# Three real products for a complex one, and an inverse transform in 64-row products over two row groups

## The chip, the cores and the metric

The kernel runs on one core of one Trainium2 chip. The metric is the time of one execution on the device, in microseconds: the median of several runs. TensorE (PE) multiplies matrices out of SBUF into PSUM, VectorE (DVE), ScalarE (ACT) and GpSimd (POOL) do elementwise work, and SyncE (SP) issues most DMAs.

## The reference

```python
def _attn_ref(x, w_r, w_i, b_r, b_i):            # x: 8 x 2496 x 256
    X = np.fft.rfft(x, axis=1)
    Yr = Xr @ w_r - Xi @ w_i + b_r               # w_r, w_i: 256 x 256
    Yi = Xr @ w_i + Xi @ w_r + b_i
    Yr = np.sign(Yr) * np.maximum(np.abs(Yr) - lam, 0.0)      # lam = 0.01, Yi alike
    y = np.fft.irfft(Y, n=x.shape[1], axis=1)
```

The result, 19968 rows of 256, goes through a mixture of 8 experts: logits `y @ w_gate`, a greedy assignment by falling logit with 2496 places for each expert, and for each expert `relu(h @ w1) @ w2` (256 to 1024 to 256).

## The kernel before, in words

The transform of 2496 = 39 x 64 points is done as matrix products, batch by batch (8 batches), in `phase_a`:

- **Stage 1** (L1063, in the last batch L1067): the 39-point transform, 11 units `u` a batch, each three products of 512 columns into a bank `p15`; ScalarE copies it out (L1083) and a DMA stores it in DRAM (`T1`).
- **Stage 2** (L1107): the 64-point transform. A step `p` (10 a batch, 80 in all) takes two frequencies k1 = 2p, 2p+1; for each, two products put the spectrum, transposed, into `ps2`: 256 channels in two halves of 128 partitions, with 64 columns of real parts and 64 of imaginary parts. The table `Ft` is the moving operand.
- Each fp32 value is then split into a high and a low fp32r part, `th` and `tl` (tiles `xTh`, `xTl`): ScalarE writes `th` (L1116), VectorE the rest `tl` (L1117). The negated imaginary part is put ahead of the real one (L1118 on ScalarE, L1119 on VectorE), so that a window of 128 columns reads (Xr, Xi) or (-Xi, Xr).
- **Stage 3** (L1126) is the complex product. For each of the two frequencies 12 products of 256 columns sum into one half of `ps3`: for w_r and w_i, for two channel halves, the three terms high-high, high-low, low-high. The 128 output partitions are 64 real and 64 imaginary rows of one frequency.
- VectorE adds the bias in place (L1132), ScalarE and VectorE apply the threshold (L1133, L1134), and the result is split again into `zh` (ScalarE, L939) and `zl` (GpSimd, L942).
- **Stage 4** (L1142): the inverse 64-point transform. For each frequency three products of 128 rows and 256 columns (table halves `Gt` high and low, data `zh` and `zl`) sum into a half of `ps4`; one ScalarE copy (L1144) and a DMA to `T2` in DRAM.
- **Stage 5** (L1173, from batch 5 on L1177): the inverse 39-point transform of the batch before, 11 units a batch, again in `p15`, copied by ScalarE (L1178), stored as rows of y. Four transposes (L1196) and small gate products (L1214, 32 columns of the array each) give the logits.

A planner (`Plan`) sets the order on every engine. Each task has an engine, a cost, a due place `pos` (10 per batch), the buffers that it reads and writes; a simulation of its own takes the task that can start first, and the instructions are emitted in that order. Rings of buffers (`RINGS`) say how many tiles a kind has: `p15=2, ps2=2, ps3=2, ps4=1`. So the work of several batches and stages is interleaved on each engine, and every engine takes its instructions strictly in the order emitted. An early part of the routing for the first half of the rows (`R.early`, L423 and L727 to L790) is planned between the places 52.5 and 78, on VectorE mostly. After the last batch the experts follow (L624 transposes, L639 first layer, L656 second layer), with the rest of the routing on VectorE beside them.

At the start, 32 products of 64 rows (L1079) run on a tile of zeros; they keep TensorE busy until data arrives and compute nothing:

```python
for i in range(2 * WARM):
    for r in range(2): T.matmul(psw[r].t, lhsT=zr.t[64 * r:64 * r + 64, 0:128], rhs=zr.t[64 * r:64 * r + 64], ...)
```

## Time and profile before

| | |
|---|---|
| runs of the kernel | 1554.78, 1556.19, 1557.17 us; median 1556.19 |
| the profiled execution | 1560.31 us, of which its span 1558.5 |
| granted TensorE clock, mean | 0.995 |
| busy | PE 1524.0, DVE 1063.4, ACT 854.4, POOL 670.0 us |
| stage 3 products | 1920, between 31.0 and 564.6 us |
| stage 4 products | 480, between 40.2 and 572.1 us |

The span runs from the first to the last instruction of the profiled execution; the rest of its time lies around it. Busy time is the union of the records of an engine. A record of PE has a modelled end, and records overlap, so the pace of products is read from one start to the next. The transform takes the first 620 us or so, and the experts the rest.

### The profile page before, as it was taken

What the parts mean: (1) busy time and instruction counts of PE and PEld (TensorE: products, weight loads), DVE (VectorE), ACT (ScalarE), POOL (GpSimd) and SP (SyncE); (2) the same over time, 40 slices, a digit from 0 to 9 for tenths busy, and PEclk for the clock granted to TensorE, in tenths of its full rate; (3) what the DMA queues carried; (4) which work ended last, traced back from release to release, by engine and by line L of the source; (5) the groups of instructions that cost most, each with busy time, mean ns of one, the idle gap of its engine ahead of it and who ended that gap; (6) DMA issues with size and microseconds to landing.
All of it is one profiled execution on the core that took longest, in us unless ns stands there. A gap on an engine that the chain in (4) does not pass through costs nothing.

```text
span 1558.5 us, 31615 instructions
## 1 busy us (share of the span) xinstructions
PE 1524.0 (98%) x10991; PEld 1363.4 (87%) x10991; DVE 1063.4 (68%) x3452; ACT 854.4 (55%) x1870; POOL 670.0 (43%) x891
## 2 busy tenths in 40 slices
PE   7999999999899999999999999999999999999998
PEld 5999999998878877888788998988988889989997
DVE  3676667676975574889989888897777765552321
ACT  2778888787678776444536234344353443552332
POOL 2246556564536444343334434334324343353332
PEclk9999999999999999999999999999999999999999
DMA  9678777877758566434213122121211212311110
GB/s 272 193 243 257 221 248 219 254 240 225 228 172 269 168 205 191 150 114 131 91 43 101 45 69 72 47 89 53 89 44 54 88 57 71 117 51 47 41 47 29
DMA packets 144201, 208.25 MB, mean 134 GB/s; under 512 B 28751, under 2 KB 108575, under 8 KB 144030
## 3 DMA queue, kind: packets, MB, share of 16 engines
q1 hardware_dynamic: 127244, 162.30, 33.9%
q0 software_dynamic: 16656, 43.77, 9.0%
q8 instruction: 89, 1.46, 0.4%
q14 instruction: 82, 0.67, 0.1%
q10 hardware_dynamic: 130, 0.06, 0.0%
HBM read 121.31 MB, written 84.75 MB: 132 GB/s over the span
## 4 chain that ended last, share of the span: by engine, by line
PE 79%; DVE 7%; issue 5%; DMA 4%; ACT 3%; POOL 2%; SPq 0%; POOLq 0%; DVEq 0%; ACTq 0%
PE ps L656 25%; PE ps L639 18%; PE ps L1126 10%; PE p L639 6%; PE ps L1107 4%; PE ps L1142 3%; PE p L1063 2%; PE p L1173 2%; PE ps L624 2%; PE both L1196 2%; PE p L1177 1%; DVE junk L423 1%; POOL out_dram L664 1%; PE ps L1214 1%; DMA sh<-in_x_dram 1%
## 5 line engine op out<-in xcount | busy, mean ns | idle before, releaser
L1126 PE MATMUL ps<-wt,xTh 128*128 128x256 f32 x1280 | 243.6, 288 | 2.2 <-DVE y L1134 1.1
L1126 PEld LDWEIGHTS ps<-wt,xTh 128*128 128x128 f32 x1280 | 198.8, 189 | 10.5 <-issue 5.9
L1126 PE MATMUL ps<-wt,xTl 128*128 128x256 f32 x640 | 178.9, 280 | 0.3 <-DVE xTl L1119 0.3
L664 POOL DMA_INDIRECT out_dram<-xTh,li x64 | 66.0, 1031 | 254.1 <-ACT xTh L660 218.9
L423 DVE SCALAR_TENSOR_TENSOR junk<-h_m,st,h_AG 128x156 bf16<-128x156 f32 (+1 forms) x472 | 160.8, 385 | 2.7
L942 POOL TENSOR_TENSOR zl<-y,zh 128x512 fp32r<-128x512 f32 x80 | 106.4, 1330 | 119.2 <-ACT zh L939 106.1
L1203 POOL TENSOR_TENSOR yTl<-yr,yTh 128x468 bf16<-128x468 f32 (+1 forms) x88 | 96.9, 1103 | 117.7 <-ACT yTh L1202 113.6
L1126 PEld LDWEIGHTS ps<-wt,xTl 128*128 128x128 f32 x640 | 120.5, 188 | 0.5 <-DVE xTl L1119 0.5
L656 PE MATMUL ps<-FG,yTh 128*128 128x256 f32 (+1 forms) x472 | 107.4, 282 | 0.0
L664 POOL DMA_INDIRECT out_dram<-xTl,li x64 | 65.3, 1020 | 91.9 <-ACT xTl L660 75.9
L1107 PE MATMUL ps<-FG,sh 128*128 128x128 f32 x640 | 98.0, 281 | 4.8 <-DMA sh<-T 4.3
L1107 PEld LDWEIGHTS ps<-FG,sh 128*128 128x128 f32 x640 | 87.3, 194 | 13.4 <-DMA sh<-T 4.8
L660 ACT COPY xTl<-ps 128x256 f32<-128x256 f32 x80 | 29.8, 372 | 126.0 <-PE ps L656 96.5
L660 ACT COPY xTh<-ps 128x256 f32<-128x256 f32 x80 | 29.9, 374 | 123.0 <-PE ps L656 95.6
L942 POOL TENSOR_TENSOR s2l<-s2c,s2h 120x512 fp32r<-120x512 f32 (+2 forms) x60 | 77.1, 1288 | 42.6 <-DVE s2h L939 31.1
L656 PE MATMUL ps<-FG,y 128*128 128x256 f32 x408 | 84.7, 282 | 0.0
L942 DVE TENSOR_TENSOR xl<-xt,xh 117x512 fp32r<-117x512 f32 (+1 forms) x66 | 65.4, 992 | 24.9 <-ACT xh L939 22.9
L1117 DVE TENSOR_TENSOR xTl<-ps,xTh 128x512 fp32r<-128x512 f32 x80 | 54.8, 685 | 40.0 <-ACT xTh L1116 39.3
L656 PEld LDWEIGHTS ps<-FG,yTh 128*128 128x128 f32 (+1 forms) x472 | 77.8, 186 | 1.1
L656 PE MATMUL ps<-FG,s1st 128*128 128x256 f32 (+1 forms) x356 | 74.2, 284 | 0.0
L656 PE MATMUL ps<-FG,yst 128*128 128x256 f32 x328 | 72.6, 282 | 0.0
L1201 DVE TENSOR_TENSOR yr<-both,yTh 128x468 f32<-128x468 f32 (+1 forms) x77 | 48.1, 625 | 35.9 <-ACT yTh L1200 33.0
(699 smaller groups left out, 5054.7 us busy)
## 6 DMA issues: line engine op xcount, KB each, us to landing
xt<-in_moe_w_dram SPq DMA_DIRECT2D x64, 512.0 KB
T<-s4st SPq DMA_DIRECT2D x80, 256.0 KB
sh<-T SPq DMA_DIRECT2D x39, 512.0 KB
s2c<-T SPq DMA_DIRECT2D x80, 240.0 KB
YD<-yst SPq DMA_DIRECT2D x80, 234.0 KB
T<-s1st SPq DMA_DIRECT2D x73, 240.0 KB
xt<-in_x_dram SPq DMA_DIRECT2D x105, 156.0 KB
sh<-in_x_dram SPq DMA_DIRECT2D x14, 156.0 KB
```

Source lines behind the costliest of these rows:

```text
L423: v(cols + 59 + 1400 * K.extra, p, lambda k=k: V.scalar_tensor_tensor(junk[k % 2].t[:, 0:cols], H.m[:, 0:cols], c.t[:, k // ng:k // ng + 1 ...
L639: T.matmul(ps.t[:, 0:w], lhsT=W1.t[:, a, m, 128 * ft:128 * ft + 128], rhs=x_.t[:, 0:w], start=q + m == 0, stop=q + m == 3)
L656: T.matmul(ps.t[0:M], lhsT=a.t[:, 128 * q:128 * q + M], rhs=W2.t[:, w_, ft], start=k == 0, stop=k == 23)
L660: plan.add('A', .27, pos + 1, lambda: A.copy(o.t[0:M], ps.t[0:M]), [ps], [o])
L664: ins = P.indirect_dma_start(out=self.out, out_offset=bass.IndirectOffsetOnAxis(ap=oi.t[0:M, oo + t:oo + t + 1], axis=0), in_=o.t[0:M], in ...
L942: lambda: eng.tensor_tensor(lb[1](), src(), hb[1](), op=OP.subtract), [srcb, hb[0]], [lb[0]])
L1107: T.matmul(ps.t[:, i, 128 * dt:128 * dt + 128], lhsT=sh.t[:, k, 128 * dt:128 * dt + 128], rhs=Ft.t[:, k], start=True, stop=True)
L1117: plan.add('V', dve(512), pos, lambda th=th, tl=tl, src=src, apart=apart: apart(V.tensor_tensor(cols(tl, 64, 192), src(), cols(th, 64, 192 ...
L1126: T.matmul(ps3.t[:, i], lhsT=a.t[:, i, dt, o:o + 128], rhs=wt[c].t[:, w, dt], start=n == 0, stop=n == 11)
L1142: T.matmul(ps4.t[:, i], lhsT=Gt[p // 8].t[:, g, (2 * p + i) % 16], rhs=v.t[:, i], start=n == 0, stop=n == 2)
L1201: plan.add('V', dve(2 * W), pos + 0.376, lambda yh=yh, yr=yr, psT=psT, W=W: V.tensor_tensor(yr.t[:, :, 0:W], psT.t[:, :, 0:W], yh.t[:, 0, ...
L1203: yq.append(plan.add('P', pool(2 * W), pos + 0.376, lambda yh=yh, yl=yl, yr=yr, W=W: P.tensor_tensor(yl.t[:, :, 0:W], yr.t[:, :, 0:W], yh. ...
```

## The change

Stage 3 computes with three real products in place of four. With S = Xr + Xi it forms Xr (w_i - w_r), S w_r and -Xi (w_r + w_i); then Yr is the second plus the third, Yi the second plus the first. Each is a group of 6 products of 256 columns (two channel halves, three terms) for both frequencies of the step at once: the 128 stationary columns are now 64 of one frequency and 64 of the other. The groups go into the two halves of `ps3`: the first into half 1; the second into half 0; VectorE reads half 0 out into `sk`, with b_i added (L1150), and only then the third group sums onto half 0. Two adds of VectorE finish: b_r to half 0 (L1157), `sk` to half 1 (L1158). S itself is formed from the two split parts: an add on VectorE (L1135), a second one of two SBUF operands (L1137, on GpSimd for even steps and on VectorE for odd ones; batch 0 all on VectorE), then split by ScalarE (L1138) and GpSimd (L1139). The negated part and its split go away. The weight sums are formed once at the start, with one more split (tile kinds `w3h`, `w3l`).

So real and imaginary parts of both frequencies now lie in the two halves of one tile, and stage 4 takes 64 rows at a time: 12 products a step in place of 6, alternating between the rows 0 to 63 (first frequency, one bank) and 64 to 127 (second frequency, another bank); two copies of 256 columns in place of one of 512. The table `Gt` is arranged to suit, through the stationary columns of `Ft`, which stage 2 now reads as two pieces of 64 columns.

To hold this, `ps4` has two banks and `p15` one (with `ps4` in its place for every second unit of the last batch), some buffers are laid out anew, and `R.early` is planned from place 52.5 to 98.

The core of the diff:

```diff
-            th, tl = sb("xTh", [128, 2, 2, 192], F32R), sb("xTl", [128, 2, 2, 192], F32R)
+            th, tl = sb("xTh", [128, 3, 4, 64], F32R), sb("xTl", [128, 3, 4, 64], F32R)
...
-                        T.matmul(ps.t[:, i, 128 * dt:128 * dt + 128], lhsT=sh.t[:, k, 128 * dt:128 * dt + 128], rhs=Ft.t[:, k], start=True, stop=True)
+                        T.matmul(ps.t[:, 2 * dt + i], lhsT=sh.t[:, k, 128 * dt:128 * dt + 128], rhs=Ft.t[:, k // 2 * 2:k // 2 * 2 + 2, 64 * (k % 2):64 * (k % 2) + 64], start=True, stop=True)
...
-            plan.add('A', act(256, False), pos + .01, lambda th=th, apart=apart: apart(A.mul(cols(th, 0, 64), cols(th, 128, 192), -1.0)), [th_], [th])
-            plan.add('V', dve(256), pos + .01, lambda th=th, tl=tl, src=src: V.tensor_tensor(cols(tl, 0, 64), cols(th, 128, 192), src(64), op=OP.subtract), [ps, th_], [tl])
+            plan.add('V', dve(256), pos + .01, lambda th=th, sq=sq, src=src: V.tensor_tensor(sq(), src()[:, 0], th.t[:, 1].bitcast(F32), op=OP.add), [ps, th_] + ([Bsk] if b + p else []), [Bk] + ([] if b + p else [Bsk]))
+            s1_, s2_ = vb(), vb()
+            plan.add(*(('V', dve(256)) if p % 2 or not b else ('P', pool(256))), pos + .01, lambda tl=tl, sq=sq, e=(P, V)[p % 2 or not b]: e.tensor_tensor(sq(), sq(), tl.t[:, 1].bitcast(F32), op=OP.add), [Bk, tl_], [s1_], uses=[Bsk, Bk])
+            plan.add('A', act(256, False), pos + .02, lambda th=th, sq=sq: A.copy(th.t[:, 2], sq()), [s1_], [th, s2_], uses=[Bsk, Bk])
+            plan.add(*(('P', pool(256)) if b else ('V', dve(256))), pos + .02, lambda th=th, tl=tl, sq=sq, e=P if b else V: e.tensor_tensor(tl.t[:, 2], sq(), th.t[:, 2].bitcast(F32), op=OP.subtract), [s1_, s2_], [tl, sl_], uses=[Bsk, Bk])
...
-                                T.matmul(ps3.t[:, i], lhsT=a.t[:, i, dt, o:o + 128], rhs=wt[c].t[:, w, dt], start=n == 0, stop=n == 11)
+                            T.matmul(ps3.t[:, o], lhsT=a.t[:, x_, 2 * dt:2 * dt + 2].rearrange("p q k -> p (q k)"), rhs=w_at[w_](w)[:, dt], start=n == 0 and k < 2, stop=n == 5, skip_group_check=k == 2)
...
+                if k == 2:
+                    Bk2 = vb()
+                    plan.add('V', dve(256), pos + .8, lambda ps3=ps3, sk=sk: V.tensor_tensor(sk(), ps3.t[:, 0], Bbt.t[:, 1], op=OP.add), [b0, Bbt], [Bk, Bk2], uses=[ps3, Bsk])
+                    need = [Bk2]
+                plan.add('T', .71, pos + .7 + .15 * k, mm3, need + w_of[w_], [ps3, got], uses=[th, tl])
...
-            plan.add('V', dve(512), pos + 1.282, lambda ps3=ps3: V.tensor_tensor(ps3.t, ps3.t, bt[:, None, :].to_broadcast([128, 2, 256]), op=OP.add), [ps3, Bbt], [yb], uses=[ps3])
+            plan.add('V', dve(256), pos + 1.282, lambda ps3=ps3: V.tensor_tensor(ps3.t[:, 0], ps3.t[:, 0], Bbt.t[:, 0], op=OP.add), [ps3, Bbt], [yb], uses=[ps3])
+            plan.add('V', dve(256), pos + 1.282, lambda ps3=ps3, sk=sk: V.tensor_tensor(ps3.t[:, 1], ps3.t[:, 1], sk(), op=OP.add), [ps3, Bk2], [yb], uses=[ps3, Bsk, Bk])
...
-                for i in range(2):
-                    for n, (g, v) in enumerate(((0, zh), (0, zl), (1, zh))):
-                        T.matmul(ps4.t[:, i], lhsT=Gt[p // 8].t[:, g, (2 * p + i) % 16], rhs=v.t[:, i], start=n == 0, stop=n == 2)
+                for n in range(6):
+                    c, (g, v) = n % 2, ((0, zh), (1, zh), (0, zl))[n // 2]
+                    for i in range(2):
+                        T.matmul(ps4[i].t, lhsT=Gt[p // 8].t[64 * i:64 * i + 64, g, (2 * p + c) % 16], rhs=v.t[64 * i:64 * i + 64, c], start=n == 0, stop=n == 5)
...
-                 FG=2, fg=1, wt=2, eq=1, T1=2, T2=2, p15=2, ps2=2, ps3=2, ps4=1, pt=1, pc=1, lo=1, hs=6, ho=1,
+                 FG=2, fg=1, wt=2, eq=1, T1=2, T2=2, p15=1, ps2=2, ps3=2, ps4=2, pt=1, pc=1, lo=1, hs=6, ho=1,
...
-                R.early(Pos(52.5, 78, 128), Ft)
+                R.early(Pos(52.5, 98, 128), Ft)
```

What this makes of the order on PE. Before, a stretch of the first batch: stage 2 (L1107), a whole stage 4 (L1142), then the two weights of one frequency in stage 3 (`wt_367` is w_r, `wt_372` is w_i), one right behind the other.

```order
L1107 MATMUL ps_1374<-FG_238,sh_1050 128x128 x2
L1142 MATMUL ps_1377<-zh_1338,FG_359 128x256
L1142 MATMUL ps_1377<-zl_1356,FG_359 128x256
L1142 MATMUL ps_1377<-zh_1338,FG_359 128x256 x2
...
L1126 MATMUL ps_1388<-wt_367,xTh_1314 128x256 x2
L1126 MATMUL ps_1388<-wt_367,xTl_1334 128x256
...
L1126 MATMUL ps_1388<-wt_372,xTh_1314 128x256 x2
L1126 MATMUL ps_1388<-wt_372,xTl_1334 128x256
```

Now, in a steady batch, the second group (`wt_367`, w_r) and the third (`wt_379`, the weight sum) of one step, into the same `ps_2271`:

```order
L1146 MATMUL ps_2271<-wt_367,xTh_2246 128x256 x2
L1146 MATMUL ps_2271<-wt_367,xTl_2256 128x256
...
L1126 MATMUL ps_2319<-FG_237,sh_2119 128x128 x2
L1082 MATMUL p_2365<-xh_2287,d_94 120x512
L1082 MATMUL p_2365<-xl_2315,d_94 120x512
...
L1146 MATMUL ps_2271<-wt_379,xTh_2246 128x256 x2
L1146 MATMUL ps_2271<-wt_379,xTl_2256 128x256
```

Between the two groups the planner has put half a stage 2 (L1126 in the new numbering) and a unit of stage 1 (L1082), the time in which VectorE reads the bank out.

Stage 4 in the new order on PE, between a unit of stage 5 (L1200) and stage 2: `ps_2297` and `ps_2298` are the banks of the two frequencies.

```order
L1200 MATMUL p_2283<-s2h_2159,d_95 39x256
L1169 MATMUL ps_2297<-zh_2254,fg_563 128x256
L1169 MATMUL ps_2298<-zh_2254,fg_563 128x256
...
L1169 MATMUL ps_2297<-zl_2266,fg_563 128x256
L1169 MATMUL ps_2298<-zl_2266,fg_563 128x256
...
L1126 MATMUL ps_2319<-FG_237,sh_2119 128x128 x2
```

The 12 products of a step stand together, the two row groups in turn, with products of the whole array ahead of them and behind.

VectorE around the same step, in the new order. L1150 is the read-out of `ps_2271`, L1137 an add of two SBUF operands, L953 the low part of a stage-1 input (also two SBUF operands):

```order
L1133 TENSOR_TENSOR xTl_2295<-ps_2258,xTh_2279 128x512
L1135 TENSOR_TENSOR sk_411<-ps_2258,xTh_2279 128x256
L953 TENSOR_TENSOR xl_2315<-xt_1863,xh_2287 117x512
L1137 TENSOR_TENSOR sk_411<-sk_411,xTl_2295 128x256
L1230 TENSOR_TENSOR yr_2363<-both,yTh_2356 128x2x156
L1150 TENSOR_TENSOR sk_411<-ps_2271,bt_346 128x256
L953 TENSOR_TENSOR xl_2371<-xt_1863,xh_2359 117x512
L1157 TENSOR_TENSOR ps_2271<-ps_2271,bt_346 128x256
L1158 TENSOR_TENSOR ps_2271<-ps_2271,sk_411 128x256
```

The read-out stands behind two adds of SBUF operands and a subtraction that waits for the transposes (L1230); before, no VectorE instruction stood between products of the same step.

## Rows read from the trace of the kernel before

**Rows 1.** The page: busy time of each engine, and the chain that ended last.

```profile
PE 1524.0 (98%) x10991; PEld 1363.4 (87%) x10991; DVE 1063.4 (68%) x3452; ACT 854.4 (55%) x1870; POOL 670.0 (43%) x891
...
PE 79%; DVE 7%; issue 5%; DMA 4%; ACT 3%; POOL 2%; SPq 0%; POOLq 0%; DVEq 0%; ACTq 0%
```

**Rows 2.** Windows: busy us (instructions), then PE clock, DMA share, GB/s.

```profile
154.00:221.00 67.00, 67.00 (x558) 62.08 (x558) 45.92 (x74) 54.82 (x111) 40.26 (x33) 1.00 0.80 238
...
289.00:357.00 68.00, 68.00 (x568) 63.08 (x566) 45.93 (x74) 55.78 (x112) 40.65 (x34) 1.00 0.78 243
357.00:439.00 82.00, 76.27 (x604) 66.75 (x603) 69.34 (x209) 59.42 (x118) 40.14 (x34) 1.00 0.70 209
620.00:1540.00 920.00, 914.01 (x6178) 825.08 (x6177) 647.93 (x2619) 388.03 (x905) 359.15 (x598) 1.00 0.23 73
```

The engines in a row of these windows stand in the order PE, PE's weight loads, DVE, ACT, POOL.

**Rows 3.** Waits of PE from 154 to 357 us: total us, times, longest.

```profile
PE both L1196 <- ACT yst L1178: 0.6, 1, 0.6
```

**Rows 4.** Timeline of PE, 300.2 to 302.2 us: start, length, instruction.

```profile
300.08 0.40 PE L1126 MATMUL ps<-wt,xTh 128*128 128x256 f32 x2
300.31 0.28 PE L1126 MATMUL ps<-wt,xTl 128*128 128x256 f32 x1
300.52 0.48 PE L1214 MATMUL ps<-yTh,wg 128*32 128x234 bf16 x10
...
301.24 0.39 PE L1142 MATMUL ps<-zh,FG 128*128 128x256 f32 x1
301.47 0.28 PE L1142 MATMUL ps<-zl,FG 128*128 128x256 f32 x1
```

**Rows 5.** Timeline of all engines, 310.2 to 311.4 us.

```profile
310.26 0.39 PE L1173 MATMUL p<-s2h,d 120*117 120x512 f32 x1
...
310.69 0.58 ACT L1178 COPY yst<-p 117x512 f32<-117x512 f32 x1 [0.63 <-PE p L1173]
...
311.17 0.59 ACT L1116 CAST xTh<-ps 128x512 fp32r<-128x512 f32 x1
```

**Rows 6.** The page: groups of stage 3; busy us, mean ns, idle before.

```profile
L1126 PE MATMUL ps<-wt,xTh 128*128 128x256 f32 x1280 | 243.6, 288 | 2.2 <-DVE y L1134 1.1
...
L1126 PE MATMUL ps<-wt,xTl 128*128 128x256 f32 x640 | 178.9, 280 | 0.3 <-DVE xTl L1119 0.3
```

**Rows 7.** Timeline of PE, 17.83 to 21.6 us: the warm-up and what follows.

```profile
18.35 2.17 PE L1079 MATMUL ps<-xh 64*128 64x256 f32 x32
20.45 1.22 PE L1080 MATMUL ps<-xh 128*128 128x256 f32 x8
21.50 0.27 PE L983 MATMUL ps<-yr,FG 128*128 128x128 f32 x1
```

**Rows 8.** Groups of VectorE by line and form, 154 to 357 us.

```profile
L1132 DVE TENSOR_TENSOR ps<-ps,bt 128x512 f32<-128x512 f32 x30 | 20.8, 693 | 4.6 <-PE ps L1126 4.6
...
L1119 DVE TENSOR_TENSOR xTl<-xTh,ps 128x256 fp32r<-128x256 f32 x30 | 12.2, 407 | 0.0
```

**Rows 9.** Line 942 on VectorE and GpSimd, 154 to 357 us: ns min/median/max.

```profile
L942 DVE TENSOR_TENSOR xl<-xt,xh x33: 681/1156/1794, 155.3 to 342.7; 117x512 fp32r<-117x512 f32 x30, 78x512 fp32r<-78x512 f32 x3
...
L942 POOL TENSOR_TENSOR s2l<-s2c,s2h x36: 725/1290/1769, 166.7 to 353.7; 120x512 fp32r<-120x512 f32 x30, 120x256 fp32r<-120x256 f32 x3, 40x256 fp32r<-40x256 f32 x3
```

**Rows 10.** Groups of ScalarE over the whole span.

```profile
L1144 ACT COPY s4st<-ps 128x512 f32<-128x512 f32 x80 | 46.9, 586 | 17.4 <-PE ps L1142 16.8
...
L660 ACT COPY xTh<-ps 128x256 f32<-128x256 f32 x80 | 29.9, 374 | 123.0 <-PE ps L656 95.6 <-PE both L434 18.9 <-issue 5.8
```

**Rows 11.** Timeline of VectorE, 300.2 to 301.4 us.

```profile
300.63 0.70 DVE L1132 TENSOR_TENSOR ps<-ps,bt 128x512 f32<-128x512 f32 x1 [0.48 <-PE ps L1126]
```

**Rows 12.** Timeline of all engines, 248 to 249.3 us.

```profile
248.41 0.58 ACT L1178 COPY yst<-p 117x512 f32<-117x512 f32 x1
...
249.04 0.52 PE L1196 MATMUL both<-h_idn,yst 117*128 117x117 f32 x3 [0.57 <-ACT yst L1178]
```

More of the change, by code (lines that the diff above doesn't have):

```diff
@@ L69, in route_consts, with pair0 @@
     return r
+def pair0(G, two):
+    g = np.stack([np.concatenate([G[64 * c:64 * c + 64, k] for k in range(2)]) for c in range(2)], 1)
+    return np.ascontiguousarray(two(g).transpose(1, 0, 2, 3))
 def const_arrays():
@@ L921, in phase_a @@
     wt = [sb("wt", [128, 2, 2, 256], F32R) for _ in range(2)]
+    w3 = [sb(k, [128, 2, 256], F32R) for k in ("w3h", "w3l")]
+    w_at = [lambda a, i=i: wt[i].t[:, a] for i in range(2)] + [lambda a: w3[a].t]
+    w_of = [[wt[0]], [wt[1]], w3]
+    Bbt, Bsk = sb("bt", [128, 2, 256]), sb("sk", [128, 2, 256])
+    Bs = [Buf(None, None, True) for _ in range(2)]
     Bd1.state = Bd5.state = Bwg.state = False
@@ L963, in gate @@
             b = gates[key]
[L964 removed]
+            return [plan.add('P', 0.15, -99 if key in (at(0), at(6)) else -50, lambda: P.tensor_copy(spacer[0:1, 0:1], b.t[0:1, 0, 0:1] if key[0] == 's1st' else b.t[0:1, 0, 0, 0:1].bitcast(F32)), [b])]
         for q, (k0, k1) in enumerate(FQ):
@@ L1052, in batch @@
             if 0 < b < F1: h, l = [sb(k, [117, 2, 256], F32R) for k in ("xh", "xl")]
-            ps = psum("p15", [120, 2, 256])
+            ps = psum("p15" if b or u % 2 else "ps2", [120, 2, 256])
             st = gates['s1st', b, u] = sb("s1st" if b else ("s1st", "s4st", "yst", "s2c")[u % 4], [120, 2, 256])
@@ L1111, in apart @@
-            def apart(ins, two=two):
-                for other in two: K.tc.declare_no_dep(ins.ins, other.ins, reason="distinct columns")
-                two.append(ins)
-            cols = lambda x, a, b: x.t.rearrange("p i t k -> p (i t) k")[:, :, a:b]
-            src = lambda a=0, ps=ps: ps.t.rearrange("p i (t k) -> p (i t) k", t=2)[:, :, a:128]
-            plan.add('A', act(512), pos, lambda th=th, src=src: A.copy(cols(th, 64, 192), src()), [ps], [th, th_])
-            plan.add('V', dve(512), pos, lambda th=th, tl=tl, src=src, apart=apart: apart(V.tensor_tensor(cols(tl, 64, 192), src(), cols(th, 64, 192), op=OP.subtract)), [ps, th_], [tl])
@@ L1129, in batch @@
-            y, t, zh, zl = sb("y1", [128, 2, 256]), sb("y2", [128, 2, 256]), sb("zh", [128, 2, 256], F32R), sb("zl", [128, 2, 256], F32R)
+            th_, tl_, sl_ = vb(), vb(), vb()
+            src = lambda ps=ps: ps.t.rearrange("p q (c k) -> p c q k", c=2)
+            sk, Bk = lambda p=p: Bsk.t[:, p % 2], Bs[p % 2]
+            plan.add('A', act(512), pos, lambda th=th, src=src: A.copy(th.t[:, 0:2], src()), [ps], [th, th_])
+            plan.add('V', dve(512), pos, lambda th=th, tl=tl, src=src: V.tensor_tensor(tl.t[:, 0:2], src(), th.t[:, 0:2], op=OP.subtract), [ps, th_], [tl, tl_])
@@ L1161, in batch @@
             if b < F5: h, l = sb("s2h", [120, 2, 256], F32R), sb("s2l", [120, 2, 256], F32R)
-            ps = psum("p15", [117, 2, 256])
+            ps = psum("ps4" if b == NB - 1 and u % 2 else "p15", [117, 2, 256])
             st = sb("yst", [117, 2, 256])
@@ L1188, in batch @@
             W = 234 if u < 10 else 156
-            psT = psum("p15" if b == NB - 1 else "pt", [128, 2, 234])
-            yh, yl, yr = sb("yTh", [128, 2, 2, 234], BF), sb("yTl", [128, 2, 234], BF), sb("yr", [128, 2, 234])
+            psT = psum(("ps4", "p15")[u % 2] if b == NB - 1 else "pt", [128, 2, 234])
+            yh, yr = sb("yTh", [128, 2, 2, 234], BF), sb("yr", [128, 2, 234])
+            if not u % 2: yl = sb("yTl", [128, 2, 2, 234], BF)
+            yv = lambda yl=yl, u=u: yl.t[:, u % 2]
             def tr(u=u, st=st, psT=psT):
```

66 lines of the change are left out of this document (37 added, 29 removed).

## The prediction

> **What bounds the kernel now.** I read the page's totals first, then the windows by stage, then who TensorE waits for. The page has TensorE busy for 98% of a span of 1558.5 us, and the chain that ended last runs through PE for 79% [rows 1]. A share over the whole span is an average, so the windows come next: for a batch in the middle of the transform stretch (67 and 68 us each) PE is busy throughout at full clock, VectorE 46, ScalarE 55, GpSimd 40 us; in the experts' stretch of 920 us PE is busy 914 [rows 2]. In 203 us of steady batches PE waits once, 0.6 us [rows 3]. So both halves are bound by TensorE and what is saved there should come out at the end, if nobody else becomes late. The one weak place is the stretch 357 to 439, where the early routing is on VectorE too: DVE 69 of 82 us, PE 5.7 us idle [rows 2].
>
> A PE row's 0.28 us is no price: it includes the pipeline, and the next product starts before it ends. The price is the distance of two starts. In a run of stage 3 the third start comes 0.23 us after the first, so **0.118 us** for 256 columns [rows 4]. In the same way a ScalarE copy recorded with 0.58 us is followed by the next after 0.48 [rows 5], so busy shares of ScalarE and VectorE overstate how full they are.
>
> **The change, part by part.** (1) *Three products for four.* Stage 3 has 1280 + 640 = 1920 products [rows 6], 24 in each of 80 steps; the change issues 3 x 6 = 18. 480 fewer x 0.118 = **-56.6 us** on the bound engine.
>
> (2) *Stage 4 in two row groups.* Six products of 128 rows become 12 of 64 rows, in pairs. If a pair costs two products, that alone is 480 x 0.118 = +56.6 and the change gives nothing. The start of this very kernel holds the answer: the warm-up's 32 products of 64 rows, alternating over two row groups and two banks, take from 18.35 to 20.45, 2.10 us for 16 pairs [rows 7]; 16 x 0.118 would be 1.89. A pair costs one product. But there is a remainder, 0.21 us, and after it the eight 128-row products take 1.05 us where 0.94 is due: 0.11 more. Entering is seen at the gate's 32-column products: 0.21 from the last stage-3 start to the first of them, 0.09 more than 0.118 [rows 4]. Together a detour into another array shape costs 0.09 + 0.21 + 0.11 = **0.41 us**. The gate alone shows 0.09 going in and, coming out, 0.23 between the first two stage-4 products where 0.118 is due, so at least 0.20 [rows 4]. In the changed order all 80 stage-4 blocks stand among products of the full array: 80 x 0.41 = **+32.8 us**, bounds 16 and 33. I take the upper one, since the warm-up is the same kind of product.
>
> The Trainium skill (TensorE: Matmul & The Clock Gate, Part 3, the span model) gives a packed set the span of one product and some 4 ns for each further tile, and puts no price on changing shape; by it the sum would be without the 32.8. Another page (TensorEngine Tiling (Array Packing), Tiling Modes) says that a change of mode drains the engine, with no figure. The remainders of [rows 4, 7] agree with the second, and the case without them is a rival below.
>
> (3) *Work that moves to the other engines.* Per step VectorE loses the negated part (0.41) and the 512-wide bias add (0.69) and gains the sum of both parts (0.41), every second step an add with both inputs in SBUF, the read-out between the products (0.41) and two 256-wide adds instead of one (0.81) [rows 8]. The SBUF add is not in the trace at 256 columns; half of the 512-wide one's least and median gives 0.34 to 0.58 [rows 9], 0.29 per step at the upper end, which I take since GpSimd will be busier. Net +0.8 us a step, +8 a batch: 46 becomes 54. GpSimd gains 1.5 adds of 256 columns at 0.74 (725 ns is the least that its row shows [rows 9]): +11 a batch, 40 becomes 51. ScalarE swaps a negation for a copy of the same size and one 512 copy (0.59) for two of 256 (0.37): +0.16 a step [rows 10], 55 becomes 57. A batch on PE becomes 67.5 - 7.1 + 4.1 = 64.5 us, so the three stand at 84, 79 and 88%: still under PE, and I cost this work at **nothing** where it only has to keep up. The cover is the other stages' PE work; without it the whole of the 0.8 us a step, 64 us, would show.
>
> (4) *A new wait inside each step.* The third group adds into the bank that holds the second, so VectorE must first read it out. From the last product's start to a waiting VectorE it takes 0.32 us (300.31 to 300.63) [rows 4, 11], the read-out 0.41 [rows 8], PE's restart about 0.05 (ACT ends 248.99, PE starts 249.04) [rows 12]: 0.77, less the product's own 0.118, so 0.65 us of other PE work must stand between. With the paces above the new order has 1.4 us there in the median; 8 steps of 80 have less and are short by **1.8 us** together.
>
> (5) *One bank p15 for two.* After a stage-1 or stage-5 block the copy starts 0.43 us after the last product's start (310.26 to 310.69) [rows 5], takes 0.59, and PE may then restart: 0.43 + 0.59 + 0.05 - 0.235 = 0.84 us of other work is needed. In the order 7 of some 160 successions have less, short by **3.0 us**. The alternation with ps4 in the last batch covers the tail.
>
> (6) *Start, routing, rest.* Three weight splits for two and their combinations are about four more VectorE instructions of 0.7 us ahead of the first step, where the spectrum still has to come back from DRAM: 0 to 3 us, I take 0. Early routing is spread to place 98 instead of 78, which thins it out on VectorE: -5.7 us if the idle time of 357 to 439 goes, 0 if the fuller VectorE keeps it; I take 0. From shortly after the last gate products on, PE's order is unchanged. DMA bytes stay but for some 0.3 MB of constants at the start.
>
> **Sum:** -56.6 + 32.8 + 1.8 + 3.0 = **-19.0 us**. The profiled execution took 1560.3, which becomes 1541.3; it stands 4.1 above the median of the runs, 1556.2, so the median becomes **1537**.
>
> **Rivals.** *A: the change of shape costs nothing* where other work stands around it. -56.6 + 4.8: 1504. For it: inside the warm-up pairs run without any loss. Against it: the extra 0.09 at every entrance and 0.11 after every exit, in the gate's rows as in the warm-up's. 4%. *B: pairs don't run side by side* on real data, or drain each time: 32.8 more than the gain at 118 ns, so +56.6 - 56.6 + 32.8 + 4.8 = +37.6: 1594. Only that the warm-up multiplies zeros speaks for it. 3%. *C: the VectorE read-out is late* and PE waits in the step. VectorE takes its queue in order; the add of two SBUF operands, 0.68 us at least, takes 1.16 in the median and 1.79 at most [rows 9], in a stretch where GpSimd works 60% of the time, and the change gives both engines more of these. A read-out behind such an add is up to 1.11 us late. The order's slack is 1.4 - 0.65 = 0.75 us, so PE would wait up to 0.36 a step, 80 x 0.36 = +29, net +10: 1566. It decides from 0.24 us a step on, which is 19 us. Against it: PE hardly waits now with ScalarE at 82%. 8%. The Trainium skill (SBUF, Who interferes with whom) has such an add of VectorE and a GpSimd operation that reads SBUF exclude each other for a whole instruction; the spread 0.68 to 1.79 agrees, and rival C is what that would do here. *D: half of C*, gain mostly eaten, within 0.2%: 1556, 9%. *The forecast*, a gain of 3 to 42 us: 76%.
>
> **Numbers.** A measurement of this kernel tells 0.2%, 3.1 us, from no change. Faster: the forecast and A, 0.80; same: D, 0.09; slower: B and C, 0.11. The range's low end has the lower bound of the shape change and the routing's idle time gone: 1537 - 16.8 - 5.7 = 1515. Its high end takes in the head's 3 us and reaches to the middle of D, 1556. It leaves out A, B, C and half of D, 0.2.
>
> **What would show it.** Right: stage-3 records fall from 1920 to 1440 and stay 0.118 apart; stage-4 pairs start some 4 ns apart and 0.118 from pair to pair, with 0.4 us lost at the edges; batches of about 64 us; PE's waits on VectorE, GpSimd and ScalarE under 10 us more than now; experts' stretch unchanged and starting some 20 us earlier. Wrong: batches of 60 us (A), stage-4 products 0.118 apart one by one (B), waits of the third group on the bias add or of the second on GpSimd in most steps (C).

## The result and the profile after

The change is **slower**: 1578.1 us (median of 4 runs, 1577.4 to 1580.8) against 1556.4 for the kernel before in the same session, a ratio of 1.0146 [1.0130, 1.0162]. The forecast was 1537. So 41 us lie between forecast and result, and the sign is wrong. The profiled run took 1580.8 us with a span of 1579.0, at a mean granted clock of 0.990 (before 0.995).

The page of the changed kernel, busy time and chain, to be set beside [rows 1]:

```profile
PE 1512.8 (96%) x10989; PEld 1317.8 (83%) x10989; DVE 1162.9 (74%) x3670; ACT 857.6 (54%) x1951; POOL 762.3 (48%) x996
...
PE 71%; DVE 12%; issue 5%; ACT 5%; DMA 4%; POOL 2%; SPq 0%; POOLq 0%; DVEq 0%; ACTq 0%
```

VectorE has 100 us more than before and GpSimd 92, and on the chain VectorE's share has gone from 7 to 12%. The windows of the batches and of the experts' stretch, to be set beside [rows 2] (same columns):

```profile
166.00:235.00 69.00, 65.74 (x562) 56.28 (x562) 59.76 (x99) 55.06 (x121) 54.35 (x49) 1.00 0.79 244
235.00:307.00 72.00, 67.73 (x567) 58.50 (x566) 59.99 (x105) 56.32 (x123) 55.35 (x50) 0.98 0.76 231
307.00:379.00 72.00, 66.31 (x558) 56.24 (x557) 60.29 (x101) 55.76 (x122) 54.50 (x47) 1.00 0.75 228
379.00:460.00 81.00, 71.00 (x576) 58.18 (x575) 73.11 (x181) 54.88 (x118) 52.34 (x49) 0.98 0.63 193
650.00:1560.00 910.00, 905.55 (x6148) 819.29 (x6147) 645.18 (x2615) 384.88 (x899) 355.52 (x594) 1.00 0.23 74
```

The experts' stretch is as it was. The last stage-3 product starts 26.2 us later than before (590.8 for 564.6): 3.1 of that stand ahead of the first batch, 5.8 in it, 12.7 in the four steady batches behind it and 4.5 in the rest; 5.7 are won back after it. The loss lies in the batches: 69 to 72 us where 67 to 68 was and 64.5 was forecast, with PE idle for 3 to 6 us of each, VectorE at 60 (forecast 54) and GpSimd at 54 to 55 (forecast 51). The waits of PE from 166 to 379 us, to be set beside [rows 3], where 0.6 us stood:

```profile
PE ps L1146 <- DVE sk L1150: 5.4, 5, 1.9
PE ps L1146 <- DVE y L1160: 1.8, 2, 1.4
PE both L1225 <- DVE yr L1230: 1.4, 1, 1.4
PE ps L1243 <- DVE y L1160: 1.3, 1, 1.3
PE both L1225 <- ACT yst L1205: 1.1, 3, 0.5
```

L1150 is the read-out between the products, L1160 the threshold, L1230 the low part behind the transposes: three different results of VectorE, all late. The last line is a copy by ScalarE. How a late one comes about is seen on three timelines around 253 us. VectorE:

```profile
249.82 0.42 DVE L1137 TENSOR_TENSOR sk<-sk,xTl 128x256 f32<-128x256 f32 x1
250.15 1.52 DVE L950 CAST s2h<-s2c 120x512 fp32r<-120x512 f32 x1
251.60 1.76 DVE L953 TENSOR_TENSOR xl<-xt,xh 117x512 fp32r<-117x512 f32 x1
253.28 0.41 DVE L1150 TENSOR_TENSOR sk<-ps,bt 128x256 f32<-128x256 f32 x1
```

GpSimd in the same time:

```profile
249.98 1.41 POOL L953 TENSOR_TENSOR s2l<-s2c,s2h 120x512 fp32r<-120x512 f32 x1 [1.66 <-DVE s2h L950]
251.35 1.46 POOL L953 TENSOR_TENSOR zl<-y,zh 128x512 fp32r<-128x512 f32 x1
252.77 1.17 POOL L1139 TENSOR_TENSOR xTl<-sk,xTh 128x256 fp32r<-128x256 f32 x1
```

And PE, which waits 1.46 us for the read-out and then makes a detour into stage 4:

```profile
251.90 0.39 PE L1082 MATMUL p<-xh,d 117*120 117x512 f32 x1
253.75 0.50 PE L1146 MATMUL ps<-wt,xTh 128*128 128x256 f32 x2 [1.46 <-DVE sk L1150]
...
254.56 0.61 PE L1126 MATMUL ps<-FG,sh 128*128 128x128 f32 x4
255.09 0.74 PE L1169 MATMUL ps<-zh,FG 64*128 64x256 f32 x8
255.67 0.39 PE L1169 MATMUL ps<-zl,FG 64*128 64x256 f32 x4
255.99 0.49 PE L1200 MATMUL p<-s2h,d 120*117 120x512 f32 x1
```

VectorE has three operations on SBUF ahead of the read-out. The cast (1.52 us) ends 0.28 us after GpSimd's first subtract (249.98 + 1.41 = 251.39), the low part behind it (1.76 us) 0.55 us after GpSimd's second (252.81), as if each had stood still until then; the read-out, which reads PSUM, takes its 0.41. Over the same 213 us this is the rule. Of the 30 casts of this size 8 took 410 to 428 ns; each of the other 22 began while an operation of GpSimd ran and ended 279 to 288 ns after that one did. Of the 15 adds of two SBUF operands (L1137) 6 took 408 to 426 ns, and the other 9 ended 277 to 284 ns after an operation of GpSimd. The 60 adds with one operand in PSUM and the result in SBUF (L1135, L1150) all took 404 to 425, whatever GpSimd did. In the kernel before, 24 of the 30 casts were of the short kind and 6 of the long. The groups of VectorE:

```profile
L953 DVE TENSOR_TENSOR xl<-xt,xh 117x512 fp32r<-117x512 f32 x32 | 35.6, 1119 | 4.4 <-ACT xh L950 4.3
L950 DVE CAST s2h<-s2c 120x512 fp32r<-120x512 f32 x30 | 26.7, 889 | 1.3 <-DMA s2c<-T 0.6 <-POOL xTl L1139 0.5
...
L1137 DVE TENSOR_TENSOR sk<-sk,xTl 128x256 f32<-128x256 f32 x15 | 13.8, 918 | 0.1
...
L1150 DVE TENSOR_TENSOR sk<-ps,bt 128x256 f32<-128x256 f32 x30 | 12.4, 414 | 2.8 <-PE ps L1146 2.8
```

The new add of two SBUF operands takes 918 ns (forecast 0.34 to 0.58), more than twice a read-out of the same size; and the cast, which the change doesn't touch, takes 889 where 549 was, since more of the casts begin while GpSimd works.

The Trainium skill (SBUF — State Buffer, Who interferes with whom) says that VectorE's casts can run in a two-port mode, and that in this mode VectorE and GpSimd shut each other out for a whole instruction; it also says that operations of VectorE with two SBUF inputs contend with GpSimd's reads. The ends above agree with it; the prediction had applied it to the adds and not to the cast.

### The profile page after: what moved, and what is told of

It reads as the page before. It is cut to its first block, busy times and chain, and to the rows that moved or that the text cites. A ratio compares the mean times of both kernels' runs of the same rounds, so it can differ in the third digit from the quotient of the medians.

```text
span 1579.0 us, 32012 instructions
## 1 busy us (share of the span) xinstructions
PE 1512.8 (96%) x10989; PEld 1317.8 (83%) x10989; DVE 1162.9 (74%) x3670; ACT 857.6 (54%) x1951; POOL 762.3 (48%) x996
## 4 chain that ended last, share of the span: by engine, by line
PE 71%; DVE 12%; issue 5%; ACT 5%; DMA 4%; POOL 2%; SPq 0%; POOLq 0%; DVEq 0%; ACTq 0%
PE ps L662 26%; PE ps L645 19%; PE p L645 6%; PE ps L1146 6%; PE ps L1126 3%; PE ps L1169 2%; PE ps L630 2%; DVE xl L953 2%; DMA xt<-in_x_dram 1%; PE p L1200 1%; PE both L1225 1%; PE p L1082 1%; PE p L1204 1%; DVE xTl L1133 1%; DVE y L1160 1%
## 5 line engine op out<-in xcount | busy, mean ns | idle before, releaser
L953 POOL TENSOR_TENSOR zl<-y,zh 128x512 fp32r<-128x512 f32 x80 | 112.4, 1405 | 94.2 <-ACT zh L950 83.6
L1146 PE MATMUL ps<-wt,xTh 128*128 128x256 f32 x640 | 134.1, 302 | 12.5 <-DVE sk L1150 12.0
L1146 PEld LDWEIGHTS ps<-wt,xTh 128*128 128x128 f32 x640 | 102.6, 191 | 36.0 <-DVE sk L1150 21.0
L1126 PE MATMUL ps<-FG,sh 128*128 128x128 f32 x640 | 96.2, 285 | 8.9 <-DMA sh<-T 8.4
L1126 PEld LDWEIGHTS ps<-FG,sh 128*128 128x128 f32 x640 | 85.1, 196 | 17.2 <-DVE wg L1028 7.7
L1146 PE MATMUL ps<-wt,xTl 128*128 128x256 f32 x320 | 90.8, 284 | 2.2 <-DVE xTl L1139 1.7
L953 POOL TENSOR_TENSOR s2l<-s2c,s2h 120x512 fp32r<-120x512 f32 (+2 forms) x60 | 76.7, 1281 | 12.8 <-DVE s2h L950 10.0
L662 PE MATMUL ps<-FG,yTh 128*128 128x256 f32 (+1 forms) x372 | 82.4, 281 | 0.0
L645 PE MATMUL ps<-yTh,sh 128*128 128x512 f32 (+1 forms) x205 | 73.6, 387 | 0.0
L953 DVE TENSOR_TENSOR xl<-xt,xh 117x512 fp32r<-117x512 f32 (+1 forms) x66 | 65.7, 1000 | 9.0 <-ACT xh L950 8.5
L1139 POOL TENSOR_TENSOR xTl<-sk,xTh 128x256 fp32r<-128x256 f32 x70 | 59.1, 847 | 20.6 <-ACT xTh L1138 19.8
L1159 ACT ACTIVATE y<-ps,ml 128x512 f32<-128x512 f32 x80 | 55.5, 694 | 21.5 <-DVE ps L1158 18.9
L662 PE MATMUL ps<-FG,s2c 128*128 128x256 f32 (+1 forms) x320 | 65.0, 281 | 0.0
L1146 PEld LDWEIGHTS ps<-wt,xTl 128*128 128x128 f32 x320 | 60.8, 190 | 3.5 <-DVE xTl L1139 2.5
```

The source lines that it names most:

```text
L645: T.matmul(ps.t[:, 0:w], lhsT=W1.t[:, a, m, 128 * ft:128 * ft + 128], rhs=x_.t[:, 0:w], start=q + m == 0, stop=q + m == 3)
L662: T.matmul(ps.t[0:M], lhsT=a.t[:, 128 * q:128 * q + M], rhs=W2.t[:, w_, ft], start=k == 0, stop=k == 23)
L953: lambda: eng.tensor_tensor(lb[1](), src(), hb[1](), op=OP.subtract), [srcb, hb[0]], [lb[0]])
L1126: T.matmul(ps.t[:, 2 * dt + i], lhsT=sh.t[:, k, 128 * dt:128 * dt + 128], rhs=Ft.t[:, k // 2 * 2:k // 2 * 2 + 2, 64 * (k % 2):64 * (k % 2) ...
L1139: plan.add(*(('P', pool(256)) if b else ('V', dve(256))), pos + .02, lambda th=th, tl=tl, sq=sq, e=P if b else V: e.tensor_tensor(tl.t[:, ...
L1146: T.matmul(ps3.t[:, o], lhsT=a.t[:, x_, 2 * dt:2 * dt + 2].rearrange("p q k -> p (q k)"), rhs=w_at[w_](w)[:, dt], start=n == 0 and k < 2, ...
```

## The experiments

Theory 1: VectorE runs late as a whole, through the operations between SBUF operands that the change adds there and on GpSimd, and what TensorE saves is lost in waiting. Theory 2: the read-out inside the step costs, whatever VectorE's load. Theory 3: the single bank p15. In the summary, "batch" is the mean distance of the first stage-3 products of neighbouring batches, second to eighth; "idle" is PE's summed idle time in that stretch per batch. Both are worked out from the traces; the batch with the early routing is among them.

```
kernel                              ratio [95%]              batch  idle
before                              1                         70.1   1.6
the change                          1.0146 [1.0130, 1.0162]   73.3   5.8
x1 no wait for the read-out         1.0245 [1.0215, 1.0275]   74.5   5.9
x2 sum by ScalarE                   1.0058 [1.0039, 1.0077]   69.2   3.3
x3 stage 4 with full rows           1.0146 [1.0118, 1.0174]   73.1   7.2
x4 planner's costs as measured      1.0174 [1.0138, 1.0209]   73.2   5.2
x5 x2 and x3                        1.0003 [0.9992, 1.0015]   68.8   5.1
x6 x2, detours merged               1.0042 [1.0023, 1.0061]   70.3   4.9
x7 x2, routing at 78                1.0086 [1.0063, 1.0108]   71.0   3.8
x8 x5, two p15                      0.9925 [0.9906, 0.9943]   69.3   5.1
x9 change, two p15 by ps3           1.0601 [1.0583, 1.0619]   81.3  11.0
x10 x2, two p15 by ps3              1.0404 [1.0389, 1.0420]   74.9   7.5
x11 before, one p15                 1.0075 [1.0061, 1.0089]   70.9   1.8
x12 change, ring of three banks     1.0115 [1.0092, 1.0137]   71.7   4.3
x13 x2, ring of three banks         1.0022 [1.0010, 1.0033]   68.7   2.6
x14 x13, detours merged             1.0020 [1.0006, 1.0034]   69.7   4.5
x15 before, y in place              1.0019 [1.0010, 1.0029]   69.8   1.7
x16 x15 with unused load            1.0096 [1.0081, 1.0112]   71.9   2.6
x17 x16, one p15                    1.0147 [1.0131, 1.0162]   71.6   2.2
```

**x1.** The third group no longer waits for the read-out:

```diff
-  ... V.tensor_tensor(sk(), ps3.t[:, 0], Bbt.t[:, 1], op=OP.add), [b0, Bbt], [Bk, Bk2], uses=[ps3, Bsk]
+  ... V.tensor_tensor(sk(), ps.t[:, 0:2].rearrange("p q k -> p (q k)"), Bbt.t[:, 1], op=OP.add), [b0, Bbt], [Bk, Bk2], uses=[ps, ps3, Bsk]
```

> The in-step read-out (L1150) adds the bias to a finished spectrum bank instead of to the second group's product, so the third group of the complex product waits for nothing; VectorE does as much work as before the edit (the second product's share is left out of the imaginary part). Theory 1 (VectorE as a whole runs late, because its two-SBUF operations and GpSimd's shut each other out): the wait moves to the next thing that VectorE hands over (bias adds, threshold, low parts), and the time falls by less than 8 us, to 1570-1578 us. Theory 2 (the dependency inside the step is what costs, whatever VectorE's load): PE's 12 us of waits at L1150 and what they push later are gone, and the time falls by 15 to 30 us, to 1548-1563 us.

1594.5 us: slower than the change, against both theories. PE's waits from 158 to 375 us:

```profile
PE ps L1146 <- DVE y L1160: 3.1, 5, 1.0
PE both L1225 <- ACT yst L1205: 3.0, 3, 2.2
PE p L1200 <- ACT s1st L1102: 1.5, 3, 0.6
PE ps L1126 <- DVE sk L1150: 1.3, 2, 0.8
```

The wait at L1146 for L1150 is gone; others stand in its place, one of them new: the read-out now holds the spectrum's bank, and the next step's transform (L1126) waits for that. The planner also moved other work, and the mean granted clock of these runs was 0.982 to 0.988, where the change had 0.990 to 0.993; that alone can account for up to 8 of the 16 us (estimate, 0.005 x 1590). So the test isn't clean and by itself rules out neither theory; x4 says more about the read-out.

**x2.** The sum with one operand in PSUM, and without L1137's SBUF add:

```diff
-  plan.add('V', dve(256), pos + .01, ... V.tensor_tensor(sq(), src()[:, 0], th.t[:, 1].bitcast(F32), op=OP.add) ...
+  plan.add('A', act(256), pos + .01, ... A.copy(sq(), src()[:, 1]) ...
-  plan.add(*(('V', dve(256)) if p % 2 or not b else ('P', pool(256))), ... e.tensor_tensor(sq(), sq(), tl.t[:, 1].bitcast(F32), op=OP.add) ...
+  plan.add('V', dve(256), ... V.tensor_tensor(sq(), src()[:, 0], sq(), op=OP.add) ...
```

> The sum of real and imaginary spectrum is made by one ScalarE copy of the imaginary part (256 columns, PSUM to SBUF, about 0.38 us) and one VectorE add that reads PSUM and that copy (about 0.41 us); the second add with two SBUF operands (L1137, 40 on VectorE at 918 ns, 40 on GpSimd at 771 ns) is gone. Per batch VectorE loses about 4.6 us of 60 and GpSimd 3.9 of 55, ScalarE gains 3.8 of 56. Theory 1 (VectorE late behind two-SBUF operations): 10 to 30 us faster than the change, 1548-1568 us. Theory 2 (the read-out dependency alone): within 4 us of the change, 1574-1582 us. Theory 3 (the single bank of stage 1 and 5): no change, or slower, since ScalarE empties that bank and has more to do.

1567.1 us, a ratio 0.0088 below that of the change, some 14 us, as Theory 1 has it. VectorE's groups from 158 to 360 us:

```profile
L950 DVE CAST s2h<-s2c 120x512 fp32r<-120x512 f32 x30 | 21.3, 710 | 3.0 <-issue 2.7 <-DMA s2c<-T 0.3
...
L1137 DVE TENSOR_TENSOR sk<-ps,sk 128x256 f32<-128x256 f32 x31 | 12.9, 415 | 1.4 <-ACT sk L1135 1.4
```

The add with an operand in PSUM takes 415 ns, and the untouched cast has come from 889 down to 710. PE's largest wait there is now 1.8 us for L1230, and the one at L1150 has gone from 5.4 to 0.6. A batch is 4 us shorter, and the last stage-3 product starts 28 us earlier; of these, 7 are lost again up to the last gate product (65.0 us for 58.3) and 7.5 behind it.

**x3.** Stage 4 without the 64-row shape:

```diff
-  ... T.matmul(ps4[i].t, lhsT=Gt[p // 8].t[64 * i:64 * i + 64, g, (2 * p + c) % 16], rhs=v.t[64 * i:64 * i + 64, c], ...
+  ... T.matmul(ps4[i].t, lhsT=Gt[p // 8].t[:, g, k], rhs=v.t[:, i], start=n == 0, stop=n == 2)
```

> Stage 4 with 6 products of 128 rows in place of 12 of 64, in the same order on every engine: no detour into the 64-row shape (half of each sum is left out). TensorE's work falls by about 0.36 us in each of 80 steps, 28.5 us. If the detour's price is on the path as the prediction had it (TensorE bounds the batches): 25 to 30 us faster, 1548-1553 us. Theory 1 (VectorE and the waits on it set the pace of a batch): a third or less of it comes through, 1568-1578 us.

1578.9 us, ratio 1.0146: 25 to 28.5 us of TensorE work are gone (25 by the medians of the blocks in this trace, 28.5 by the estimate above) and the time has **not** changed. The windows, as above:

```profile
163.00:230.00 67.00, 63.55 (x496) 55.50 (x496) 57.49 (x99) 54.12 (x120) 53.88 (x49) 1.00 0.78 241
230.00:302.00 72.00, 66.29 (x503) 59.21 (x501) 59.60 (x105) 55.29 (x121) 55.07 (x49) 0.95 0.76 235
302.00:373.00 71.00, 63.40 (x497) 55.57 (x496) 59.96 (x100) 55.79 (x122) 54.19 (x46) 1.00 0.76 235
```

PE is busy for 64.4 us of a mean 70 where it was 66.6 of 71, its idle time has grown (7.2 us a batch for 5.8), and VectorE, ScalarE and GpSimd read as in the change. TensorE's work does not set a batch of the change. The clock can have taken back a part: the runs of x3 had 0.984 to 0.988 in the mean, those of the change 0.990 to 0.993, some 9 us at most (estimate, 0.0055 x 1578), not 25.

**x4.** The planner gets the measured costs (`.9`, `.88`, `1.1` and so on for SBUF operands).

> The planner is given the durations that the trace shows for what VectorE and GpSimd do between SBUF operands (cast 0.87, low part 1.1, second add 0.9 on VectorE; low parts 1.4 and 0.88 and second add 0.8 on GpSimd, in place of 0.34, 0.60, 0.34 and 1.2, 0.69, 0.69), from the second batch on; the work is the same and only its order moves. Theory 1 with the order at fault (TensorE is put in front of what VectorE cannot have ready): 5 to 20 us faster, 1558-1573 us. Theory 1 with the load at fault (VectorE has too much to do wherever it stands): within 5 us. Theory 2: within 5 us.

1587.4 us, no faster; the interval overlaps the change's. The three runs near 1588 had a mean granted clock of 0.988; the fourth, at 0.993, took 1579.4, as the change. In the new order PE hardly waits for the read-out any more (here L1152, stage 3 is L1148), from 165 to 375 us:

```profile
PE ps L1148 <- DVE sk L1152: 0.6, 1, 0.6
```

That was 5.4 us in the change, and still the three batches take 71, 69 and 70 us where the change took 69, 72 and 72. So Theory 2 can't be the main cause, and an order made with truer costs doesn't help. Whether it is the load is tested in x16.

**x5, x6, x7, x8**, all on x2. x5 adds x3's edit. x6 issues stage 4 for two steps together. x7 is one number:

```diff
-                R.early(Pos(52.5, 98, 128), Ft)
+                R.early(Pos(52.5, 78, 128), Ft)
```

x8 is x5 with `p15=2` and `ps4=1`, stage 4 writing both halves of one bank.

> x2_sum_by_scalar with stage 4 as 6 products of 128 rows (half of each sum is left out): the same 28.5 us of TensorE work leaves that changed nothing in x3_full_rows. Theory 1 (VectorE set the pace of the change, and with its second add gone TensorE is nearer to being the bound again): now a good part of it comes through, 10 to 25 us below x2's 1567, 1542-1557 us. If something else than VectorE and TensorE set the pace (the single bank, transfers), again nothing: 1564-1570 us.

1560.0, 0.0055 below x2, 8.6 us: with VectorE relieved a third of what stage 4 saves comes through.

> x2_sum_by_scalar with stage 4 of two steps issued together, each step with its own half of the two banks: 40 detours into the 64-row shape in place of 80. At 0.38 us each that is 15.2 us of TensorE work. If that work is on the path once VectorE is relieved: 8 to 15 us below x2's 1567, 1552-1559 us. Rival: the pair holds both sets of zh and zl and both banks for longer, ScalarE and VectorE stand behind them, and the gain is given back: 1564-1575 us.

1566.7, some 2.5 us below x2 by the ratios, inside the intervals. 15 us less TensorE work, and no gain that can be told.

> x2_sum_by_scalar with the routing due from position 78 in place of 98, as before the change. Between the last product of the spectrum and the last gate product x2 takes 65.0 us and the kernel before 51.9 (of these about 5 us are expert products that x2 has issued by then and the kernel before has not). If the due time of the routing does that: 4 to 8 us below x2's 1567, 1559-1563 us. If not: 1565-1570 us, or slower where the routing's VectorE work comes into the last batches.

1574.8, 0.0028 above x2, some 4 us, with intervals that overlap: place 98 is not part of the loss, and whether it gains anything isn't shown.

> x5_sum_full_rows with stage 4's results in one bank and the second bank given back to stages 1 and 5, as before the change (output as in x5: half of stage 4's sum is left out). The difference to x5 is the price of the single bank, which the prediction put at 3.0 us. Theory 3 (the single bank sets the pace): 10 us or more below x5. The prediction: 2 to 5 us below x5. If stage 4's single bank costs more than it gives back: level with x5 or above it.

1548.6, 0.0078 below x5, 12 us: the second bank is worth four times the prediction's 3.0. The batches are as long as x5's; in the traces most of the gain lies between the last stage-3 product and the last gate product (x5 557.0 to 621.3, x8 557.1 to 613.7).

**x9, x10.** The second bank given back, with stage 4's second row group in the step's own stage-3 bank (`(ps4, ps3)[i].t[:, 0]`).

> The change with its second bank given back to stages 1 and 5 (their tiles placed as before the change); stage 4's second row group writes into the step's own stage-3 bank, which is read out by then, so all products, shapes and the complete sum stay. Against the change at 1578 us (1.0146 of the kernel before): if the single bank costs about 12 us, as x8 against x5 says, 1563-1570 us (1.004-1.009). If the prediction's 3.0 us held: 1573-1577 us. If the stage-3 bank, held longer, makes stage 3 wait: 1578 us or more.

> The edits of x2_sum_by_scalar and x9_change_two_p15 together. If VectorE's load and the single bank are separate costs (11 and 12 us): 1578 - 23 = 1555 us, level with the kernel before within 4 us (0.996-1.002). If relieving both lets TensorE's saved 26 us through: 1535-1550 us (below 0.995). If they are one and the same wait seen twice: as x2 alone, 1563-1568 us (1.004 or more).

1652.4 and 1621.6: far slower, batches of 81 and 75 us. In x9 PE waits for stage 4's copies before stage 3 and the gate (L1171, 9.4 and 5.1 us) and for VectorE before the transform (13.3 us). The stage-3 bank has no time to spare, and the bank's price can't be had this way.

**x11.** The kernel before with only the bank moved (`p15=1`, `ps4=2`, first and last batch placed as in the change).

> The kernel before with only the bank moved: one bank for stages 1 and 5, two for stage 4, and the tiles of the first and last batch placed as in the change; all arithmetic as before. The prediction's step on the bank: 3.0 us, 1.001 to 1.003 of the kernel before. If the single bank costs the 12 us of x8 against x5 by itself: 1.006 to 1.010. If it costs only where VectorE and ScalarE are loaded as in the change: below 1.002.

1.0075, 11.7 us. The single bank costs this where nothing else is changed. PE's idle time hardly grows (1.8 for 1.6 us a batch), so most of it isn't in waits that the trace names; for copies out of p15 PE waits 1.0 us in all. The group of the untouched cast, 157 to 361 us, shows that the new order also changes what VectorE runs into:

```profile
L939 DVE CAST s2h<-s2c 120x512 fp32r<-120x512 f32 x30 | 27.3, 911 | 4.5 <-DMA s2c<-T 3.0 <-POOL yTl L1203 0.9 <-PE p L1173 0.5
```

911 ns, as long as in the change, though VectorE and GpSimd have no operation more than before and GpSimd is busy for 60% of the stretch as before. 16 of the 30 casts end about 0.28 us behind an operation of GpSimd, where 6 did. So the cast's growth is a matter of when it starts, and not of the added operations alone; the bank's price and VectorE's lateness may in part be one thing.

**x12, x13, x14.** One ring of three banks for stages 1, 4 and 5 (`p15=3`), on the change, on x2, and on x6's edits.

> The change with one ring of three banks for stages 1, 4 and 5 (stage 4 takes two in turn, stages 1 and 5 one) in place of one bank for stages 1 and 5 and two for stage 4; tiles of the first and last batch as before the change; same arithmetic. Against the change (1.0146 of the kernel before): if the single bank is worth the 10 to 12 us of x11 and of x8 against x5: 1.006-1.010. If VectorE's load alone sets the pace of the change: 1.012-1.016. If stage 4 now waits for banks that stages 1 and 5 hold: above 1.016.

> x2_sum_by_scalar with the ring of three banks. VectorE's share (11 us) and the bank's share (10 to 12 us) both taken out of the change: 0.996-1.001 of the kernel before. If also the routing and the head come back and TensorE's 26 us get through: below 0.99. If bank and VectorE are one wait: 1.004-1.007, as x2.

> x13_sum_pool_of_three with the detours of two steps merged as in x6_detours_merged (40 in place of 80, 15.2 us of TensorE work). With VectorE and the bank relieved, if TensorE bounds again: 8 to 15 us below x13. If the waits still set the pace: within 4 us of x13, as x6 was of x2 (2.5 us).

1.0115, 1.0022 and 1.0020. The ring gives back 4.8 us on the change (the intervals just overlap) and 5.6 on x2, so load and bank add up, in part. x13 and x14 are the best complete versions of the change; neither beats the kernel before. Merged detours give nothing again.

**x15, x16, x17.** The kernel before, with the threshold written in place; then with operations as the change adds them, whose results nobody reads; then with x11's bank too:

```diff
+            if b:
+                half = lambda x: x.t[:, :, 0, 64:192].bitcast(F32)
+                plan.add(*(('V', dve(256)) if p % 2 else ('P', pool(256))), pos + .01, ... e.tensor_tensor(o.t, half(th), half(tl), op=OP.add), ...
+                plan.add('P', pool(256), pos + .02, ... P.tensor_tensor(dm[0].t, half(th), half(tl), op=OP.subtract), ...
```

> The kernel before with one thing of the change: the thresholded spectrum is written over the relu's result (y = t), so that two tiles serve where four did; all else as before. Control for the next run. The prediction gave this nothing: within 0.2% of the kernel before. If two buffers are too few: 1.003 or more.

> x15_before_y_in_place with the operations added between SBUF operands that the change adds, and nothing that waits for them: from the second batch on, in each step a subtract of 256 columns on GpSimd and an add of 256 columns on VectorE (odd steps) or GpSimd (even steps), their results unused. Theory 1 (these operations make VectorE late, by their own time and by shutting out or being shut out by GpSimd's): 6 to 20 us above x15, 1.004-1.013. The prediction's step 3 (VectorE and GpSimd have room in a batch): within 3 us of x15. If it is the chain of the sum that hurts and not the load: within 3 us of x15 too, and then x2's gain is that of a shorter chain.

> x16_before_with_load with the single bank of x11_before_one_p15 as well. If load and bank add up: x16 + 10 to 12 us. If they are one wait: x16 + 0 to 5 us. If the loaded engines make the bank worse (its copies wait longer): x16 + 15 us or more.

1.0019, 1.0096 and 1.0147. Two buffers for four cost 3 us. The load costs 12 us (0.0077) though nothing reads its results: what hurts is that VectorE's and GpSimd's other work comes later. In the traces the four steady batches from the second on lose 1.5 to 2.2 us each, and the batch with the early routing, where VectorE goes from 84 to 91% busy, 5.6 (87.4 for 81.8). The groups of VectorE in x15, 157 to 361 us:

```profile
L940 DVE CAST s2h<-s2c 120x512 fp32r<-120x512 f32 x30 | 16.5, 549 | 3.6 <-PE p L1175 3.6
```

And in x16:

```profile
L940 DVE CAST s2h<-s2c 120x512 fp32r<-120x512 f32 x30 | 19.8, 660 | 4.0 <-PE p L1179 3.2 <-DMA xt<-in_x_dram 0.5 <-POOL yTl L1209 0.3
...
L1123 DVE TENSOR_TENSOR dm<-xTh,xTl 128x256 f32<-128x256 f32 x15 | 10.3, 686 | 0.0
```

The cast grows from 549 to 660 ns through work that has nothing to do with it: 12 of the 30 end behind GpSimd, where 6 did. The bank adds 8 us more (0.0051). x17 has none of TensorE's savings and none of the detours, and is as slow as the change.

## Why the prediction was wrong, by its steps

**What bounds the kernel.** "What is saved there should come out at the end, if nobody else becomes late" was true of the kernel before. The condition failed.

**(1) and (2)** held as work. Stage 3 has 1440 products, 117 to 118 ns apart; stage 4's pairs start 3 ns apart and 117 ns from pair to pair. A detour, by medians over 79 of them, costs 0.09 going in (209 ns for 118), 0.19 inside (899 ns from its first start to the next product's, for 708) and 0.10 behind it (222 for 118): 0.386 us, 30.9 in all for the forecast 32.8. But work is not time: x3 takes 25 us of it away and the time stays. So the -56.6 and the +32.8 should not have been in the sum once the batches have another bound.

**(3) is the step that failed**: the work moved to VectorE and GpSimd was put at nothing, "where it only has to keep up", and it cost 12 us by itself (x16 against x15). VectorE came to 60 us a batch and not 54, since the SBUF add took 918 ns and not 580 at most (1.7 us a batch), and since the cast, not in the sum at all, went from 549 to 889 (3.4 us a batch; x11 shows that the single bank's order alone can do this); GpSimd came to 54 to 55 and not 51. Worse than the size was the rule that 84% of a batch is room enough. Each of these engines takes its queue in order, and a read-out behind 3.1 us of stretched operations (250.15 to 253.28 above) is late however much idle time the batch holds. Taking L1137's part out of the change gives some 14 us back (x2).

**(4)** put the new wait at 1.8 us; over the whole span PE waits 12.0 us at L1150. That is the place where VectorE's lateness shows most, but where the wait was almost gone the batches were no shorter by more than a microsecond (x4).

**(5)** put the single bank at 3.0 us. It is 11.7 on the kernel before (x11), 8 on the loaded one (x17 against x16), 12 in x8 against x5; the ring of three gives back about 5. It counted only successions in TensorE's order that are too close. But PE waits only 1.0 us for these copies in x11, so the price arises elsewhere: the planner puts the work of every engine in another order, VectorE's casts then run into GpSimd more (911 ns), and the last batch is another too. How much each of these does was not measured.

**(6)** The head took 3.1 us (first stage-3 product at 34.1 for 31.0), the upper end of "0 to 3, I take 0": PE waits 7.6 us for the first spectrum from DRAM, where 4.3 stood. The first batch took another 5.8 us (61.5 for 55.7, first stage-3 product to that of the next). VectorE makes the whole sum there, but that isn't shown to be why: with the same sum it took 55.7 in x1 and 56.0 in x12. The routing at 98 does no harm (x7). Not priced at all was the threshold in place: 3 us (x15).

**The sum.** y in place 3, load 12, bank 8 make 23 us, and the change lost 22. That these agree so closely is luck: x16 doesn't hold the read-out or the split bias adds, the later start (3.1 us) and part of the longer first batch stand in neither, and the lower granted clock of the change (0.990 to 0.993 by run, x17 0.994 to 0.997) can account for a few us more. So how much of the 26 us that TensorE saved has arrived is not settled: nothing by the plain sum, up to 10 if start and first batch (8.9) are costs of their own. What x3 shows is that of 25 us more the greater part would not come out.

**The rivals.** C had the mechanism, with 8%: an in-order VectorE held up by adds between SBUF operands. It had the place wrong. It looked for PE's loss in the read-out alone, from 0.24 us a step on; it is 0.15 there (12.0 / 80), and the rest stands at L1160, L1230 and the copies. It also left TensorE's gain in its sum and so came to 1566. A fell with the detours' measured price, B with the 3 ns between the products of a pair.

**Open.** With VectorE relieved and the bank back, batches stay at 66 to 69 us, and TensorE's work still comes through by a third (x5) or not at all (x14). PE then waits little and for many; which hand-over sets that pace was not found. The bank's price is only known to lie between 5 and 12 us. In most of these runs the planner laid out the order of all engines anew, so a difference holds a change of order too, whose share was not measured.
